# Attention in front of a feed-forward block on one core: the attention's small products placed on parts of TensorE's array

## The chip, the cores and the metric

The kernel runs on one core of one Trainium2 chip. The metric is device time in microseconds. The kernel before took 885.71 us (median of 3 runs, 883.98 to 885.72).

## What is computed

```python
# q, k, v: 8 batches x 8 heads x 576 x 64
kv  = einsum('bhsd,bhse->bhde', k, v)
out = einsum('bhsd,bhde->bhse', q, kv)
rms = sqrt(mean(out * out, axis=-1, keepdims=True) + 1e-06)
x   = out / rms * g_norm                 # then heads side by side: 8 x 576 x 512
h   = (x.transpose(0, 2, 1) @ U) @ V     # U: 576 x 32, V: 32 x 576, a mix along the sequence
u   = x + h.transpose(0, 2, 1)
y   = u + maximum(u @ w_ch1, 0) @ w_ch2  # 512 -> 2048 -> 512
```

The inputs are float32; U, V and the two weights come as 64-bit floats and are decoded to float32 on the chip.

## The kernel before

**The feed-forward block.** The 8 x 576 rows are cut into 9 blocks of 512 (`BLK`). A product in float32r (one pass over TensorE) is made exact enough by splitting both operands into a high and a low part: three products stand for one (`ffn1`, `ffn2`, names `uth`/`utl` for u, `ws` for weights, `hhl` for the hidden layer). The first three blocks (`NSTD`) are computed plainly; the other six, two at a time, with a Strassen scheme, whose weight forms stream from DRAM through `ring`/`ringw`, with `uT`, `uB` and `entry` as operands. While the first block is computed, the weights of each of the 16 slices are loaded, decoded (`decode`, `decode_w`: one instruction on ScalarE and four on VectorE, then a split) and written back to DRAM.

**The attention.** Heads go in pairs, 4 pairs a batch, 32 in all. A pair's steps, in order:

- `kv_step` (L287): k^T v. 512 of the 576 positions lie in `kv_sb` (four chunks of 128), the last 64 in `kvt_sb`. k and v of both heads stand side by side, so a 128x128 product gives both heads' 64x64 blocks on its diagonal; the other two blocks are waste. Batches 0 and 1 (`NATIVE`) do the tail as a product over 64 rows; later ones split the tail into high and low halves (`tails`) for one float32r product of 256 columns, and add up the two parts while copying the diagonal blocks to `kvb`.
- `out_step` (L316): q times kv. `kvb` is block-diagonal, 128x128, its off-diagonal zero, so five float32 products of 128x128 give both heads. ScalarE squares them into `x`.
- `stats_step` and `mul_step` (L329, L343): the root mean square by a chain of small instructions, and `x` scaled from PSUM.
- `xsplit_step` (L352): `x` split into `xh` (all of it, on ScalarE) and `xl` (four chunks, L136), with the low half of the tail written into the free rows of `xh` (L363).
- `turn_step` (L366): `x` transposed into `ut32`, by TensorE and an identity for batch 0, by VectorE and DRAM for the others.
- `t_step` (L382): x^T U. `u2` holds high and low halves of U, 64 columns, as the weights; nine float32r products over the four or five chunks of `xh` and `xl`.
- `t4_step` (L390): the 64 rows of the result copied to `t4` as float32r, the high part again, and the low part (L395, L396): four groups of 32 rows.
- `mix_step` (L445), for batch 0 `mix_first` and `mix_rest`: `t4` times `v4` (V's high and low parts in matching groups of rows), two products of 288 columns, added to `ut32` (L455).

**What sets the order.** Batch 0 is ordered by the table `PLAN` (tasks sorted by their places), with 12 + 10 products that keep TensorE busy. Batches 1 to 7 are placed by `PAIRS` and `STEPS` at steps of the feed-forward loop: batch 1 in the first block, 2 in the second, 3 and 4 in the third, 5 to 7 in the Strassen part; the last third of the program has no attention left. A scheduler orders the first block and the startup; from the second block on TensorE keeps the written order (`pinned`). One line, L89, records every product. Loads go by one queue (SP); `kv_sb`, `kvt_sb` and `q_sb` have one buffer each, and so has `x`.

Of the kernel before, what the change touches and what calls it, by code (L numbers as in the profile page):

```python
# [10 lines left out]
F32 = mybir.dt.float32  # L11
F32R = mybir.dt.float32r
# [38 lines left out]
PLAN = dict(pair=(0, 7, 13, 13), kv=(0, 0, 0, 0), out=(2, 0, 0, 6), stats=(2, 3, 3, 6), mul=(2, 3, 3, 6), xs=(11, 11, 10, 10), tr=(11, 11, 11, 14), t=(14, 14, 12, 14), t4=(18, 18, 14, 18), mix=(18, 23, 21, 23), mt=(42, 42, 42, 42), uv=6, v4=11, w0=49, w1=45, w2=38, w3=49, x0=49, warm=12, fill0=4, fill1=3, fill2=1, fill3=2, u2=60)  # L51
# [8 lines left out]
def build(ctx: ExitStack, tc: tile.TileContext, kv_in, kvt0_in, kvt_in, q_in, uv_in, g_in, w_in, out):  # L60
# [16 lines left out]
    x_sb = const.tile([P, NT, P], F32, name="x")  # L77
# [3 lines left out]
    u2 = const.tile([P, NT, 2 * R], F32R, name="u2")  # L81
    v4 = const.tile([P, S], F32R, name="v4")
    eps = const.tile([P, 1], F32, name="eps")
    kvb = [const.tile([P, P], F32, name=f"kvb{i}") for i in range(2)]
# [12 lines left out]
    def decode(raw, tmp, n=None):  # L97
# [8 lines left out]
        nc.vector.tensor_scalar(out=tmp, in0=tmp, scalar1=ABS_LO, scalar2=ABS_HI, op0=ALU.max, op1=ALU.min)  # L106
# [34 lines left out]

    def load_kv(b, p):
        if b == 0 and 0 < p:
            if p not in first_kvq:
                first_kvq[p] = weight_slot(f"kvq{p}", [P, 2 * MAIN + S], F32, 8 + p)
            kt = first_kvq[p][:, 0:2 * MAIN]
        else:
            kt = ldp.tile([P, 2 * MAIN], F32, name="kv_sb")
        nc.sync.dma_start(out=kt, in_=kv_in[b, p])
        if b >= NATIVE:  # L150
            tt = ldp.tile([P, 2 * P], F32, name="kvt_sb")
            nc.sync.dma_start(out=tt, in_=kvt_in[b - NATIVE, p])
            loads["t", b, p] = tt
        elif p % 2 == 0:
            if b == 0 and p > 0:
                tt = temps[:, 2 * DM:2 * DM + 2 * P]
            else:
                tt = ldp.tile([P, 2 * P], F32, name="kvt_sb")
            nc.sync.dma_start(out=tt, in_=kvt0_in[b, p // 2])
            loads["t", b, p] = loads["t", b, p + 1] = tt  # L160
        loads["kv", b, p] = kt

    def load_q(b, p):
        if b == 0 and 0 < p:
            if p not in first_kvq:
                first_kvq[p] = weight_slot(f"kvq{p}", [P, 2 * MAIN + S], F32, 8 + p)
            qt = first_kvq[p][:, 2 * MAIN:]
        else:
            qt = ldp.tile([P, S], F32, name="q_sb")
        nc.sync.dma_start(out=qt, in_=q_in[b, p])  # L170
        loads["q", b, p] = qt
# [741 lines left out]
```

## Time and profile before

| | us |
|---|---|
| median of 3 runs | 885.71 |
| profiled execution | 887.76 |
| its span | 885.8 |
| TensorE busy | 854.1 |
| VectorE busy | 637.5 |
| ScalarE busy | 385.2 |
| GpSimd busy | 154.6 |

Busy time counts the union of an engine's instructions. A product's end is drawn some way behind the start of the next one, so a busy TensorE is not one at its peak: the distance of starts tells its pace. In rows of TensorE the form 128*64 means weights of 128 rows and 64 columns, and 128x512 the moving operand. A float32 product leaves two records, a float32r one leaves one.

### The profile page before, as it was taken

How to read it: one execution, taken by the hardware profiler on the slowest of the kernel's cores; microseconds unless marked ns; L12 is line 12 of the kernel's file. 1: busy time of each engine (PE TensorE's matmuls, PEld its weight loads, DVE VectorE, ACT ScalarE, POOL GpSimd, SP SyncE). 2: the span in 40 equal slices, each digit the busy share in tenths (PEclk: the TensorE clock that was granted, in tenths of full speed). 3: DMA queues.
4: the chain of work that ended last, by engine and by line, in shares of the span. 5: the costliest groups of instructions: out<-in, count | busy, mean ns of one | idle time of the engine just before them, and what ended most of it. 6: DMA issues, size and time to landing. Idle time of an engine off the chain costs nothing.

```text
span 885.8 us, 12268 instructions
## 1 busy us (share of the span) xinstructions
PE 854.1 (96%) x4214; PEld 712.8 (80%) x4214; DVE 637.5 (72%) x1032; ACT 385.2 (43%) x673; POOL 154.6 (17%) x155
## 2 busy tenths in 40 slices
PE   7799998999998989999999999999999999999998
PEld 7687886788887878888888887788788888888886
DVE  5999997846437866749895989578756885663584
ACT  4554544333323433445554655445435434432441
POOL 2000037777886600020000000000000000000000
PEclk8899999999998999999999999999999999999999
DMA  9996676566557663158778777777676677566665
GB/s 339 406 417 263 231 246 204 159 191 193 165 161 217 208 187 113 55 177 283 221 246 285 237 225 234 257 226 225 215 207 205 200 237 239 186 194 200 194 206 171
DMA packets 111277, 195.38 MB, mean 221 GB/s; under 512 B 11120, under 2 KB 45424, under 8 KB 109296
## 3 DMA queue, kind: packets, MB, share of 16 engines
q1 hardware_dynamic: 111216, 194.60, 67.9%
q8 instruction: 34, 0.56, 0.3%
q14 instruction: 27, 0.22, 0.1%
HBM read 143.31 MB, written 51.25 MB: 220 GB/s over the span
## 4 chain that ended last, share of the span: by engine, by line
PE 76%; DVE 12%; DMA 7%; issue 3%; ACT 2%; SPq 1%; POOL 0%; DVEq 0%; ACTq 0%
PE y L89 56%; PE h L89 10%; PE pp L89 9%; DMA raw<-w_in 2%; DMA out<-st 2%; DVE dec L109 1%; DMA temps<-kvt_in 1%; DVE hhl L474 1%; DMA q_sb<-q_in 1%; DVE utl L416 1%; DVE dec L111 1%; DVE ws L117 1%; DVE ut L455 1%; DVE xh L363 1%; DVE xt L375 1%
## 5 line engine op out<-in xcount | busy, mean ns | idle before, releaser
L89 PE MATMUL y<-entry,ring 128*128 128x512 f32 x576 | 136.1, 390 | 0.0
L89 PE MATMUL y<-hhl,ws 128*128 128x512 f32 x540 | 134.4, 396 | 0.0
L89 PE MATMUL h<-uth,ws 128*128 128x512 f32 x360 | 124.1, 406 | 3.7 <-DVE hhl L474 3.6
L89 PEld LDWEIGHTS y<-entry,ring 128*128 128x128 f32 x576 | 107.4, 188 | 21.8
L89 PEld LDWEIGHTS y<-hhl,ws 128*128 128x128 f32 x540 | 101.2, 190 | 20.8
L543 DVE TENSOR_TENSOR h<-y,h 128x512 f32<-128x512 f32 x71 | 48.5, 688 | 53.4 <-PE y L89 49.0
L89 PE MATMUL y<-uB,ringw 128*128 128x512 f32 x354 | 86.1, 393 | 0.4 <-DVE st L543 0.3
L89 PEld LDWEIGHTS h<-uth,ws 128*128 128x128 f32 x360 | 69.8, 194 | 20.5 <-DVE hhl L474 6.0
L89 PE MATMUL y<-uT,ring 128*128 128x512 f32 x348 | 82.9, 391 | 0.0
L89 PEld LDWEIGHTS y<-uB,ringw 128*128 128x128 f32 x354 | 65.5, 188 | 14.3 <-DVE st L543 1.3
L89 PEld LDWEIGHTS y<-uT,ring 128*128 128x128 f32 x348 | 64.9, 188 | 13.4 <-ACT h L550 0.3
L89 PE MATMUL h<-utl,ws 128*128 128x512 f32 x180 | 72.0, 400 | 0.0
L587 DVE TENSOR_TENSOR entry<-h,entry 128x1024 fp32r<-128x1024 f32 x36 | 43.9, 1219 | 27.4 <-ACT entry L586 27.1
L473 ACT ACTIVATE hhl<-h 128x512 fp32r<-128x512 f32 x47 | 28.1, 597 | 78.3 <-PE h L89 78.2
L474 DVE SCALAR_TENSOR_TENSOR hhl<-h,hhl 128x512 fp32r<-128x512 f32 x47 | 32.2, 685 | 34.3 <-ACT hhl L473 34.1
L89 PE MATMUL y<-dec,ringw 128*128 128x512 f32 x216 | 55.5, 392 | 0.0
L89 PE MATMUL y<-hhl,ringw 128*128 128x512 f32 x216 | 55.2, 390 | 0.0
L251 POOL TENSOR_TENSOR dec<-dec 128x256 f32<-128x256 f32 x64 | 50.3, 786 | 4.9
L89 PE MATMUL y<-uT,ringw 128*128 128x512 f32 x210 | 50.7, 390 | 0.0
L586 ACT CAST entry<-h 128x1024 fp32r<-128x1024 f32 x36 | 37.9, 1053 | 25.9 <-PE y L89 25.8
L89 PEld LDWEIGHTS y<-hhl,ringw 128*128 128x128 f32 x216 | 40.5, 188 | 8.9 <-DMA ringw<-w2s 0.4
L89 PEld LDWEIGHTS y<-dec,ringw 128*128 128x128 f32 x216 | 40.0, 188 | 8.4 <-DVE dec L584 0.4
(210 smaller groups left out, 1436.1 us busy)
## 6 DMA issues: line engine op xcount, KB each, us to landing
ring<-wd SPq DMA_DIRECT2D x69, 256.0 KB, 3.7
ringw<-wd SPq DMA_DIRECT2D x66, 256.0 KB, 3.6
raw<-w_in SPq DMA_DIRECT2D x30, 512.0 KB, 10.0
wd<-ws SPq DMA_DIRECT2D x15, 1024.0 KB, 4.9
kv_sb<-kv_in SPq DMA_DIRECT2D x29, 512.0 KB, 4.5
ring<-w1s SPq DMA_DIRECT2D x48, 256.0 KB, 3.8
ringw<-w1s SPq DMA_DIRECT2D x48, 256.0 KB, 3.7
ring<-w2s SPq DMA_DIRECT2D x48, 256.0 KB, 4.1
```

The source lines that it names most:

```text
L89: ins = nc.tensor.matmul(*args, **kw)
L109: nc.vector.scalar_tensor_tensor(out=bits, in0=high, scalar=0xC0000000, in1=bits, op0=ALU.bitwise_and, op1=ALU.bitwise_or)
L111: nc.vector.scalar_tensor_tensor(out=bits, in0=low, scalar=29, in1=bits, op0=ALU.logical_shift_right, op1=ALU.bitwise_or)
L117: lo_eng.tensor_tensor(out=lo, in0=src, in1=hi.bitcast(F32), op=ALU.subtract)
L251: nc.gpsimd.tensor_tensor(out=o, in0=in0, in1=in1, op=op)
L363: nc.vector.tensor_tensor(out=xh[TAIL:P, 4], in0=s["x"][0:TAIL, 4], in1=xh[0:TAIL, 4].bitcast(F32), op=ALU.subtract)
L375: nc.vector.transpose(out=xt.rearrange("p k i j -> p i k j"), in_=x.rearrange("p i (k j) -> p i k j", j=32))
L473: nc.scalar.activation(out=hh, in_=h, func=AF.Relu)
L474: nc.vector.scalar_tensor_tensor(out=hl, in0=h, scalar=0.0, in1=hh.bitcast(F32), op0=ALU.max, op1=ALU.subtract)
L543: nc.vector.tensor_tensor(out=out, in0=in0, in1=in1, op=ALU.add)
L586: nc.scalar.copy(out=hi, in_=src)
L587: nc.vector.tensor_tensor(out=lo, in0=src, in1=hi.bitcast(F32), op=ALU.subtract)
```

## The change

- k^T v: each head gets a product of its own, with 64 columns of weights and 64 moving columns, over five chunks of 128 positions (the last one filled with zeros). The two heads write partitions 0 to 63 and 64 to 127 of one bank: two column tiles of the array, in turn. One copy moves both to `kvb`, now 128x64. The separate tails, their loads and their splits are gone; `kv_in` is padded to 640 positions.
- q times kv: each head's 64 rows of q and of `kvb` form a product of 64 rows, five a head, the heads in turn: two row tiles, each with a bank of its own.
- x^T U: `xsplit_step` and the halves of U are gone. `x` in float32 is multiplied by U with 32 columns of weights; each chunk goes to two column tiles, even chunks to tiles 0 and 2, odd ones to 1 and 3, ten products. The four groups of 32 rows then hold partial sums, and one copy moves all to `t4`, float32.
- mix: rows 0 to 63 of `t4` and `v4` give the first 288 columns, rows 64 to 127 the other 288: two row tiles, float32, each contracting the even and the odd partial sum. `v4` holds V itself, not halves, and is cleared at the start.
- `x` gets a second buffer (`x_sb[p % 2]`).
- `PLAN` loses an unused entry and gets `d`: the decoding of weight slices 1 and 2 is placed among batch 0's tasks, and their second VectorE instruction is held in the written order.

The core of the diff:

```diff
-PLAN = dict(... fill3=2, u2=60)
+PLAN = dict(... fill3=2, d=(19.5, 20))
...
-        nc.vector.tensor_scalar(out=tmp, in0=tmp, scalar1=ABS_LO, scalar2=ABS_HI, op0=ALU.max, op1=ALU.min)
+        ins = nc.vector.tensor_scalar(out=tmp, in0=tmp, scalar1=ABS_LO, scalar2=ABS_HI, op0=ALU.max, op1=ALU.min)
+        if held:
+            tc.keep_in_program_order(ins)
...
     def kv_step(b, p):
         m = loads.pop(("kv", b, p))
-        t = loads.pop(("t", b, p))
         pp = bank()
         kb = kvb[p % 2]
-        if b >= NATIVE:
-            both = sc.tile([P, 3 * P], F32R, name="tails")
...
-            mm(pp[:, 0:2 * P], lhsT=both[:, 0:P], rhs=both[:, P:], start=True, stop=False)
-        for i in range(4):
-            mm(pp[:, 0:P], lhsT=m[:, i * P:(i + 1) * P], rhs=m[:, MAIN + i * P:MAIN + (i + 1) * P],
-                             start=(i == 0 and b < NATIVE), stop=(i == 3 and b >= NATIVE))
...
+        for i in range(NT):
+            for lo in (0, D):
+                own = slice(i * P + lo, i * P + lo + D)
+                mm(pp[lo:lo + D, 0:D], lhsT=m[:, own], rhs=m[:, NT * P:][:, own], start=(i == 0), stop=(i == NT - 1))
+        move("kv", p if b == 0 else -1, kb, pp[:, 0:D])
...
-        for i in range(4):
-            mm(big[:, i * P:(i + 1) * P], lhsT=qt[:, TAIL + i * P:TAIL + (i + 1) * P], rhs=kb, start=True, stop=True)
-        small = bank()
-        mm(small[:, 0:P], lhsT=qt[:, 0:P], rhs=kb, start=True, stop=True)
+        x = x0[p] if b == 0 else x_sb[p % 2]
+        heads = [bank() for _ in range(2)]
+        for i in range(NT):
+            lo = (TAIL + i * P) % (TAIL + MAIN)
+            for k, o in enumerate(heads):
+                own = slice(k * D, k * D + D)
+                mm(o[:, i * D:(i + 1) * D], lhsT=qt[own, lo:lo + P], rhs=kb[own], start=True, stop=True)
...
-    def xsplit_step(b, p):
...
     def t_step(b, p):
-        xh, xl = state[b, p]["hl"]
+        x = state[b, p]["x"]
         tp = bank()
-        todo = [(xh, i) for i in range(NT)] + [(xl, i) for i in range(4)]
-        for n, (xx, i) in enumerate(todo):
-            mm(tp[0:2 * R, 0:P], lhsT=u2[:, i, :], rhs=xx[:, i, :], start=(n == 0), stop=(n == len(todo) - 1))
+        for i in range(NT):
+            for c in (i % 2, i % 2 + 2):
+                mm(tp[c * R:(c + 1) * R, 0:P], lhsT=u_sb[:, i, :], rhs=x[:, i, :], start=(i < 2), stop=(i >= NT - 2))
...
-        t4 = t40[p] if b == 0 and p in t40 else sc.tile([P, P], F32R, name="t4")
-        move("t4", p if b == 0 else -1, t4[0:2 * R], tp[0:2 * R, 0:P])
-        nc.scalar.copy(out=t4[3 * R:], in_=tp[0:R, 0:P])
-        nc.vector.tensor_tensor(out=t4[2 * R:3 * R], in0=tp[0:R, 0:P], in1=t4[0:R].bitcast(F32), op=ALU.subtract)
+        t4 = t40[p] if b == 0 and p in t40 else sc.tile([P, P], F32, name="t4")
+        move("t4", p if b == 0 else -1, t4, state[b, p]["tp"][:, 0:P])
...
     def keep_warm(p, n):
         for _ in range(n):
-            mm(spare, lhsT=state[0, p]["t4"], rhs=v4[:, 0:MAIN], start=True, stop=True)
+            mm(spare[:, 0:P], lhsT=state[0, p]["t4"], rhs=v4[:, 0:P], start=True, stop=True)
...
-            mm(mp, lhsT=t4, rhs=v4[:, lo:lo + n], start=True, stop=True)
+            rows = slice(lo // n * D, lo // n * D + D)
+            mm(mp, lhsT=t4[rows], rhs=v4[rows, lo:lo + n], start=True, stop=True)
...
+    ahead = 1 + len(PLAN["d"])
+    for f, place in enumerate(PLAN["d"]):
+        tasks.append((place, lambda f=f: decode_w(1 + f, True)))
```

Two places show how the instructions stand. The first is TensorE between two feed-forward products of the third block, where one pair's mix, the next one's x^T U, q times kv and k^T v stand close together (`pp` is the bank written, `t_` is `t4`, `u_` is U, `kvb` holds kv, `ws` and `hhl` belong to the feed-forward block). Before:

```order
L89 MATMUL pp<-v_101,t_2498 128x288 x2
L89 MATMUL pp<-xh,u_100 64x128 x5
L89 MATMUL pp<-xl,u_100 64x128 x4
L89 MATMUL pp<-kvb_103,q_sb 128x128 x5
L89 MATMUL y<-hhl,ws_568 128x512 x12
L89 MATMUL pp<-tails 128x256
L89 MATMUL pp<-kv_sb 128x128 x4
```

After:

```order
L89 MATMUL pp<-v_102,t_2486 128x288 x2
L89 MATMUL pp<-x_94,u 32x128 x10
L89 MATMUL pp<-kvb_104,q_sb 128x64 x10
L89 MATMUL y<-hhl,ws_567 128x512 x12
L89 MATMUL pp<-kv_sb 64x64 x10
```

The steps keep their places; the nine products of x^T U, the five of q and the five of k^T v are ten each now, and smaller.

The second is VectorE at the end of the startup, where batch 0's last pairs, the first mix (`utl`) and the decoding (`dec`, `raw_156` and `raw_149` are weight slice 1, `raw_167` is slice 2, `ws` the split slice) share the queue. Before:

```order
L347 TENSOR_TENSOR x_128<-y,r_387 128x512
L349 TENSOR_TENSOR x_128<-y,r_387 64x128
L130 CAST st<-pp 64x128
L396 TENSOR_TENSOR st<-y,st 32x128
L106 TENSOR_SCALAR dec<-dec 128x1024
L109 SCALAR_TENSOR_TENSOR dec<-raw_156,dec 128x1024
L136 TENSOR_TENSOR xhl_129<-x_128,xhl_129 128x512
L363 TENSOR_TENSOR xhl_129<-x_128,xhl_129 64x128
L396 TENSOR_TENSOR st<-pp,st 32x128
L107 TENSOR_SCALAR dec<-dec 128x1024
L111 SCALAR_TENSOR_TENSOR dec<-raw_156,dec 128x1024
L109 SCALAR_TENSOR_TENSOR dec<-raw_167,dec 128x1024
```

After:

```order
L319 TENSOR_TENSOR x_128<-y,r_393 128x5x64 x2
L106 TENSOR_SCALAR dec<-dec 128x1024
L109 TENSOR_SCALAR dec<-dec 128x1024
L387 SCALAR_TENSOR_TENSOR utl<-pp,g_sb,uth 128x512
L111 SCALAR_TENSOR_TENSOR dec<-raw_149,dec 128x1024
L387 SCALAR_TENSOR_TENSOR utl<-y,g_sb,uth 128x512
L113 SCALAR_TENSOR_TENSOR dec<-raw_149,dec 128x1024
L119 TENSOR_TENSOR utl<-ut_0_95,uth 128x64
L119 TENSOR_TENSOR utl<-ut_1_96,uth 128x64
L119 TENSOR_TENSOR ws_409<-dec,ws_409 128x4x256
```

The splits of x and the small steps of t4 are gone from between, and slice 1 is decoded to its end before slice 2 begins, where before the two were mixed.

More of the change, by code (lines that the diff above doesn't have):

```diff
@@ L59, in build @@
 @with_exitstack
-def build(ctx: ExitStack, tc: tile.TileContext, kv_in, kvt0_in, kvt_in, q_in, uv_in, g_in, w_in, out):
+def build(ctx: ExitStack, tc: tile.TileContext, kv_in, q_in, uv_in, g_in, w_in, out):
     nc = tc.nc
@@ L75, in build @@
     dram = ctx.enter_context(tc.tile_pool(name="dram", bufs=1, space=bass.MemoryType.DRAM))
-    x_sb = const.tile([P, NT, P], F32, name="x")
+    x_sb = [const.tile([P, NT, P], F32, name=f"x{i}") for i in range(2)]
     ut32 = [const.tile([P, S], F32, name=f"ut32_{c}") for c in range(ND)]
@@ L80, in build @@
     g_sb = const.tile([P, 1], F32, name="g_sb")
-    u2 = const.tile([P, NT, 2 * R], F32R, name="u2")
-    v4 = const.tile([P, S], F32R, name="v4")
+    u_sb = const.tile([P, NT, R], F32, name="u")
+    v4 = const.tile([P, S], F32, name="v4")
     eps = const.tile([P, 1], F32, name="eps")
-    kvb = [const.tile([P, P], F32, name=f"kvb{i}") for i in range(2)]
+    kvb = [const.tile([P, D], F32, name=f"kvb{i}") for i in range(2)]
     pinned = [False]
@@ L140, in build, with first_slot @@
     first_kvq = {}
+    def first_slot(p):
+        if p not in first_kvq:
+            first_kvq[p] = weight_slot(f"kvq{p}", [P, 2 * NT * P + S], F32, 8 + p)
+        return first_kvq[p]
     def load_kv(b, p):
[L143 to L148, printed above, removed]
-        nc.sync.dma_start(out=kt, in_=kv_in[b, p])
-        if b >= NATIVE:
[L151 to L160, printed above, removed]
+        kt = first_slot(p)[:, 0:2 * NT * P] if b == 0 and 0 < p else ldp.tile([P, 2 * NT * P], F32, name="kv_sb")
+        nc.sync.dma_start(out=kt, in_=kv_in[b, p])
         loads["kv", b, p] = kt
     def load_q(b, p):
[L164 to L169, printed above, removed]
+        qt = first_slot(p)[:, 2 * NT * P:] if b == 0 and 0 < p else ldp.tile([P, S], F32, name="q_sb")
         nc.sync.dma_start(out=qt, in_=q_in[b, p])
@@ L618, in build @@
     for _ in range(PLAN["warm"]):
-        mm(spare[:, 0:P], lhsT=kvb[0], rhs=kvb[0], start=True, stop=True)
+        mm(spare[:, 0:P], lhsT=v4[:, 0:P], rhs=v4[:, 0:P], start=True, stop=True)
     nc.scalar.sqrt(out=kvb[0][:, 0:1], in_=kvb[0][:, 0:1])
     x123 = weight_slot("x123", [P, NPAIR - 1, NT, P], F32, 15)
-    x0 = [x_sb] + [x123[:, p] for p in range(NPAIR - 1)]
-    xhl = weight_slot("xhl0", [P, NT + 4, P], F32R, 14)
-    xhl0 = [xhl[:, 0:NT], xhl[:, NT:]]
-    for t in x0:
-        nc.gpsimd.memset(t[TAIL:P, 4, :], 0.0)
-    nc.gpsimd.memset(kvb[1], 0.0)
+    x0 = x_sb[:1] + [x123[:, p] for p in range(NPAIR - 1)]
+    nc.gpsimd.memset(x123[:, 0, 0, 0:1], 0.0)
     make_identity(nc, ident)
-    t40 = {p: st.tile([P, P], F32R, name="st") for p in (1, 2, 3)}
+    t40 = {p: st.tile([P, P], F32, name="st") for p in (1, 2, 3)}
     early = [temps[:, i * DM:(i + 1) * DM] for i in range(2)]
@@ L633, in build @@
     for t in t40.values():
-        nc.gpsimd.memset(t[:, 0:1].bitcast(F32), 0.0)
-    for t in xhl0:
-        nc.gpsimd.memset(t[:, 0, 0:1].bitcast(F32), 0.0)
+        nc.gpsimd.memset(t[:, 0:1], 0.0)
     uvs = weight_slot("uvs", [P, DM], I64, 12)
@@ L661, in uv_step @@
         decode(uvraw, uv)
[L662 to L665 removed]
+        move("u", 0, u_sb, uv[:, 0:NT * R].rearrange("p (i r) -> p i r", r=R))
     def v4_step():
         for n in range(4):
[L669 to L670 removed]
+            for k in (n // 2 * 2, n // 2 * 2 + 1):
+                move("v4", n, v4[n * R:(n + 1) * R, k * VQ:(k + 1) * VQ], uv[k * R:(k + 1) * R, NT * R:])
     tasks = [(PLAN["uv"], uv_step), (PLAN["v4"], v4_step)]
@@ L709, in o @@
         def o():
-            for what in (out_step, stats_step, mul_step, xsplit_step):
+            for what in (out_step, stats_step, mul_step):
                 what(b, p)
```

85 lines of the change are left out of this document (21 added, 64 removed).

## The prediction

> **What bounds the kernel now.** I read first the page's busy times and its chain of work that ended last.
>
> ```profile
> PE 854.1 (96%) x4214; PEld 712.8 (80%) x4214; DVE 637.5 (72%) x1032; ACT 385.2 (43%) x673; POOL 154.6 (17%) x155
> PE 76%; DVE 12%; DMA 7%; issue 3%; ACT 2%; SPq 1%; POOL 0%; DVEq 0%; ACTq 0%
> ```
>
> TensorE is busy for 96% of the span and 76% of the chain runs over it; VectorE has 12% of the chain. Such shares are a mean over stages, so the view by windows comes next (a row: stretch, its length, then busy us of each engine with its instructions, granted clock, DMA share, GB/s).
>
> ```profile
> core 0: us, PE busy (x) PEld busy (x) DVE busy (x) ACT busy (x) POOL busy (x), PEclk, DMA share, GB/s
> 20.00:40.00 20.00, 14.38 (x106) 12.80 (x105) 18.92 (x44) 9.35 (x23) 0.61 (x1) 0.91 1.03 407
> 40.00:100.00 60.00, 57.45 (x264) 47.32 (x264) 56.06 (x76) 31.96 (x50) 0.00 (x0) 0.94 0.84 333
> 100.00:150.00 50.00, 48.73 (x251) 40.05 (x250) 47.32 (x73) 23.19 (x41) 19.46 (x14) 1.00 0.64 225
> 150.00:250.00 100.00, 96.44 (x478) 79.51 (x477) 58.52 (x99) 32.45 (x61) 80.47 (x70) 0.98 0.56 174
> 250.00:350.00 100.00, 91.92 (x490) 77.40 (x489) 65.27 (x136) 36.55 (x82) 42.37 (x37) 0.95 0.59 178
> 350.00:550.00 200.00, 199.67 (x1030) 168.23 (x1030) 158.50 (x283) 100.40 (x183) 5.18 (x4) 1.00 0.69 216
> ```
>
> Three stages: from 20 to 150 us VectorE is full (122.3 of 130 us) with the weight decoding and batches 0 and 1; from 150 to 350 us TensorE leads, with 11.6 us idle and a granted clock of 0.98 and 0.95; from 350 us on TensorE has no gap (199.67 of 200). So a VectorE instruction saved before 150 us is worth up to its length, one saved later only where TensorE waits for it, and a TensorE nanosecond added after 150 us counts in full. 24 of the 32 head pairs (batches 2 to 7) lie after 150 us.
>
> **What a pair costs TensorE now.** The timeline of TensorE, in a stage without gaps (start, length with the drawn-out end, records). The pace is the distance of starts, since the drawn lengths overlap; an fp32 product leaves two records, a float32r one leaves one.
>
> ```profile
> 403.08 0.28 PE L89 MATMUL pp<-tails 128*128 128x256 f32 x1
> 403.19 1.05 PE L89 MATMUL pp<-kv_sb 128*128 128x128 f32 x8
> 404.00 1.63 PE L89 MATMUL pp<-uT,ring 128*128 128x512 f32 x6
> 405.46 1.53 PE L89 MATMUL y<-uT,ring 128*128 128x512 f32 x6
> 406.83 2.89 PE L89 MATMUL y<-uB,ring 128*128 128x512 f32 x12
> 409.56 0.47 PE L89 MATMUL pp<-xh,u 128*64 128x128 f32 x5
> 409.86 0.41 PE L89 MATMUL pp<-xl,u 128*64 128x128 f32 x4
> 410.10 1.33 PE L89 MATMUL pp<-kvb,q_sb 128*128 128x128 f32 x10
> 411.19 1.17 PE L89 MATMUL y<-uB,ringw 128*128 128x512 f32 x4
> ```
>
> A 512-column product takes (409.56 - 406.83) / 12 = 0.227 us. k^T v: 404.00 - 403.08 = 0.92, and the six products behind it take 1.46 instead of 1.37, so 1.02 with its exit. x^T U: 410.10 - 409.56 = 0.54 for 9 records, 0.060 each, with 64 columns of weights. q times kv: 411.19 - 410.10 = 1.09, 0.109 a record, and the same 0.1 behind it: 1.18. The mix:
>
> ```profile
> 291.95 0.43 PE L89 MATMUL pp<-v,t 128*128 128x288 f32 x2
> 292.22 0.47 PE L89 MATMUL pp<-xh,u 128*64 128x128 f32 x5
> ```
>
> 0.27 for two, 0.135 each. With 0.06 for leaving x^T U (its narrow weights are followed by a full load, 0.109 against 0.060), a pair is 1.02 + 1.18 + 0.60 + 0.27 = **3.07 us**.
>
> **The change on TensorE.** Two rows that before already holds say what the parts will cost. First, products of 64 rows (the startup's ident times x and the batch 0 and 1 tails):
>
> ```profile
> 40.04 0.43 PE L89 MATMUL pp<-ident,x 64*128 64x64 f32 x2
> 40.31 0.38 PE L89 MATMUL y<-ident,x 64*128 64x64 f32 x2
> 40.63 0.30 PE L89 MATMUL y<-v,st 128*128 128x64 f32 x1
> ...
> 48.58 1.05 PE L89 MATMUL pp<-kv_sb 128*128 128x128 f32 x8
> 49.56 0.48 PE L89 MATMUL pp<-kvt_sb 64*128 64x128 f32 x2
> 49.98 0.50 PE L89 MATMUL pp<-utl,w1s 128*128 128x512 f32 x1
> 50.31 0.40 PE L89 MATMUL pp<-uth,w1s 128*128 128x512 f32 x1
> ```
>
> Of four records with 64 moving columns and 128 of weights none is quicker than one with 128: the starts are 0.27 apart for two, so over 0.11 each. I read that as the weight load setting the pace, 0.11 for 128 columns and 0.060 for 64. And entering and leaving a 64-row product costs: from 48.58, eight records at 0.109 should end at 49.45 and the two of 64 rows at 49.67, but the second 512 product starts at 50.31, where 49.90 would do: 0.4, which I take as **0.39** a visit. The 64-column block x^T U (form 128*64) was entered 2.73 us after its twelve predecessors began, so without any loss.
>
> The Trainium skill, page "TensorEngine Tiling (Array Packing)", section "Key Properties", says that changing the tiling mode, not just the tile, drains TensorE. The trace agrees for 64-row tiles (0.39 a visit) and not for 64-column ones (0.06). By that rule k^T v and x^T U would pay 0.39 as well.
>
> After, a pair if tiles overlap fully:
> - k^T v: ten products, 20 records, 64 columns of weights, two column tiles in turn: 20 x 0.060 / 2 = 0.60, exit 0.06. Bounds: 0.60 overlapped, 1.20 not.
> - q times kv: 20 records, 128 columns of weights, two row tiles in turn: 20 x 0.111 / 2 = 1.11, visit 0.39. Bounds 1.11 and 2.22.
> - x^T U: ten fp32 products, 20 records of 128 moving columns at 0.109, four column tiles: 0.55, exit 0.06. Bounds 0.55 and 2.18. The float32r split is gone, but an fp32 record streams longer; nothing is gained.
> - mix: two fp32 products of four passes at 0.135: 0.54 side by side, visit 0.39. Bounds 0.54 and 1.08.
>
> Sum 0.66 + 1.50 + 0.61 + 0.93 = 3.70, so **+0.63 us a pair**. Nothing covers it after 150 us: 24 x 0.63 = **+15.1 us**. For the four pairs of batch 1 VectorE sets the pace and I cost them at nothing (2.5 us if that cover is gone); in the startup TensorE has 5.6 of 20 us free, which hides the fp32 first mix.
>
> **The change on VectorE, before 150 us.**
>
> ```profile
> L136 DVE TENSOR_TENSOR xl<-x,xh 128x512 fp32r<-128x512 f32 x30 | 20.9, 697 | 0.0
> L363 DVE TENSOR_TENSOR xh<-x,xh 64x128 fp32r<-64x128 f32 x30 | 12.6, 420 | 0.5
> L396 DVE TENSOR_TENSOR t<-pp,t 32x128 fp32r<-32x128 f32 x29 | 8.2, 281 | 4.5 <-ACT t L395 3.9
> L136 DVE TENSOR_TENSOR u<-uvs,u 128x160 fp32r<-128x160 f32 x1 | 0.4, 425 | 0.0
> L117 DVE TENSOR_TENSOR uvs<-uvs 128x144 fp32r<-128x144 f32 x1 | 0.4, 397 | 0.0
> ...
> kv_sb<-kv_in SPq DMA_DIRECT2D x29, 512.0 KB, 4.5
> ```
>
> Three instructions go per pair, 0.697 + 0.420 + 0.281 = 1.40 us, for eight pairs 11.2; two of U and V, 0.82: 12.0 us. The scaling of x (640 columns in two instructions) and t4's move stay; the new memset stands before the first load lands. The two decodings moved ahead of the first hidden layer issue no DMA; on VectorE's queue they stand behind the last scaling of x and ahead of three utl of the first mix, as they nearly did before: nothing. Against it, a load of k and v of batch 0 grows from 512 KB (and half a 128 KB tail) by 64 KB; five stand ahead of the last early weight, 0.33 MB at the 407 GB/s of that window: 0.8 us. So **-11.2 us**, if TensorE can follow; at worst nothing.
>
> **The waits of 150 to 350 us.** A place:
>
> ```profile
> 277.30 0.69 PE L89 MATMUL pp<-xh,u 128*64 128x128 f32 x4 [2.60 <-ACT xh L124]
> 278.82 0.37 PE L89 MATMUL pp<-xh,u 128*64 128x128 f32 x1 [0.83 <-DVE xh L363]
> ...
> 281.51 0.77 PE L89 MATMUL h<-uth,ws 128*128 128x512 f32 x1
> 282.08 0.63 PE L89 MATMUL h<-utl,ws 128*128 128x512 f32 x1
> ```
>
> TensorE waits 3.4 us for the halves of x and then runs at half pace (0.57 for a 512-column product). The halves vanish, and x gets a second buffer. What is late next is x itself (the square root's chain), the q load and the stores, so not all of 11.6 us idle and 7 us of clock (100 x 0.02 + 100 x 0.05) comes back. I take **-7**; bounds 0 and -18.6.
>
> **Sum.** +15.1 - 11.2 - 7 = -3.1 us. The profiled execution took 887.76 us (span 885.8, 2.0 around it), the median run 885.71; 2.05 apart, and neither has a reason to change. 885.7 - 3.1 = **882.6 us**.
>
> **Rivals.**
> 1. *Two at a time* (slower). An fp32 product's two records go to the same tile; if the second holds up the queue behind it, only two products run at once however many tiles there are: x^T U 1.10, mix 0.81, +0.82 more a pair. 24 x 1.45 - 18.2 = +16.6: 902 us, 908 with batch 1 uncovered. It decides as soon as x^T U takes over 0.9 us. For it: no row of before has two tiles at once. The Trainium skill, page "TensorE: Matmul & The Clock Gate", section "Part 3: Packing small matmuls — row/col tiling", says that matmuls start and end strictly in program order, and also that ones on different tiles run concurrently; that is this rival.
> 2. *Loads one after another* (slower): k^T v 1.20, q 2.22, so +1.71: 24 x 2.34 - 18.2 = +38, 924 us. For it: the weight load sets the pace of these forms.
> 3. *No overlap at all*, the tiles do not do what the change says: 1.20 + 2.22 + 2.18 + 1.08 against 2.80 overlapped, +3.88: 28 x 4.51 - 18.2 = +108, 994 us.
> 4. *Every change of mode drains* (slower): 0.33 more for k^T v and for x^T U, 24 x 0.66 = +15.8, 898 us. Against it: the free entry of 64-column tiles; for it: 32-column tiles are not shown. The rule of the Trainium skill quoted above would bring this.
> 5. *All waits go*: the whole 18.6 instead of 7: 871 us.
>
> **Chances.** Forecast 0.50, with its own range 874 to 891 (0.36 faster, 0.08 within, 0.06 slower); rival 1 0.14, 2 0.10, 3 0.07, 4 0.05, 5 0.14. No change means within 0.2%, 1.8 us, about what a measurement of this kernel can tell. Faster 0.36 + 0.14 = 0.50, same 0.08, slower 0.06 + 0.14 + 0.10 + 0.07 + 0.05 = 0.42. The range takes in the forecast and rivals 1, 4 and 5 and leaves out 2 and 3 (0.17): 866 to 912.
>
> **What would show it.** In the timeline after: a block of ten kv_sb products (20 records) about 0.66 long, x^T U about 0.6 (1.1 says rival 1, 2.2 rival 3), q times kv about 1.5 with its visit (2.6 says rival 2), mix about 0.9; the last decoding on VectorE some 10 us earlier than now; TensorE's idle time between 150 and 350 us near 5 us. The forecast is wrong if a pair costs TensorE over 3.85 us, or if the first block of outputs ends no earlier.

## The result, and the profile after

The changed kernel takes 899.61 us (median of 4 runs, 898.97 to 900.96), the kernel before 884.85 us (4 runs, one more than above, 883.17 to 885.72): a ratio of 1.0171, 95% interval 1.0149 to 1.0193, so slower by 1.7%. The profiled execution took 900.01 us with a span of 898.2; before it was 887.76 and 885.8. So the spans differ by 12.4 us, and the steps below are made against that. The medians differ by 14.8: the execution of before that was profiled is 2.9 us above its median, the one of after 0.4.

The page's busy times and chain of work, after:

```profile
PE 877.0 (98%) x5308; PEld 697.8 (78%) x5308; DVE 556.1 (62%) x839; ACT 351.1 (39%) x597; POOL 148.6 (17%) x143
...
PE 74%; POOL 9%; DMA 7%; DVE 6%; ACT 2%; issue 1%; SPq 0%; DVEq 0%; POOLq 0%; ACTq 0%
```

TensorE is busy 22.9 us longer (877.0 against 854.1), VectorE 81.4 us shorter. VectorE's share of the chain is halved, 6% instead of 12%, and the kernel is slower all the same. GpSimd, which prepares the Strassen weights, now has 9% of the chain where it had none.

The view by windows, after (columns as in the prediction):

```profile
20.00:40.00 20.00, 16.33 (x191) 13.93 (x180) 14.18 (x35) 6.17 (x13) 0.61 (x1) 0.89 1.03 409
40.00:100.00 60.00, 58.25 (x380) 45.93 (x380) 58.04 (x81) 32.81 (x51) 0.00 (x0) 1.00 0.89 341
100.00:150.00 50.00, 50.00 (x280) 38.08 (x279) 42.03 (x58) 19.51 (x29) 22.62 (x18) 1.00 0.64 230
150.00:250.00 100.00, 95.14 (x596) 74.27 (x595) 38.06 (x66) 27.75 (x52) 82.72 (x73) 1.00 0.57 177
250.00:350.00 100.00, 98.54 (x751) 76.86 (x750) 43.55 (x90) 30.18 (x70) 34.13 (x31) 1.00 0.59 176
```

From 150 to 350 us TensorE's idle time fell from 11.6 to 6.3 us, and the granted clock is 1.00 in both stretches. That part went as forecast or better. The next view says where the time was lost. VectorE's addition of the residual to each output of the three plain blocks has a line of its own; its row gives the first and the last start. Before and after:

```profile
L487 DVE TENSOR_TENSOR st<-y,uth x12: 678/692/693, 155.3 to 391.0; 128x512 f32<-128x512 f32 x12
```

```profile
L444 DVE TENSOR_TENSOR st<-y,uth x12: 682/691/692, 151.9 to 391.1; 128x512 f32<-128x512 f32 x12
```

The first block's output comes 3.4 us earlier (151.9 against 155.3). The third block's last output starts at the same moment, 391.1 against 391.0. So in these two executions all gains and losses up to there cancel, and **nearly the whole 12.4 us arise behind it**, in the Strassen part (898.2 - 391.1 = 507.1 against 885.8 - 391.0 = 494.8). This part hardly changes from one profile to another (494.3 to 495.5 us in the kernels below whose Strassen part has only k^T v on tiles, 507.2 in the one that has the blocks of after), so the 2.4 us by which the medians differ further most likely lie ahead of it; no profile shows them. The twelve pairs of batches 5 to 7 stand in it, all but the first k^T v. TensorE is busy for 502.8 us of it instead of 489.2, 13.6 more, and idle for 1.3 less (4.3 instead of 5.6, given up between 550 and 690 us): 13.6 / 12 = 1.13 us more a pair, where the prediction had 0.63.

One whole pair of that part, in the timeline of TensorE, after. The 512-column products between the blocks are the feed-forward block's:

```profile
421.01 0.51 PE L89 MATMUL pp<-v,t 64*128 64x288 f32 x1
421.02 0.51 PE L89 MATMUL h<-v,t 64*128 64x288 f32 x1
421.36 0.40 PE L89 MATMUL pp<-v,t 64*128 64x288 f32 x1
421.37 0.40 PE L89 MATMUL h<-v,t 64*128 64x288 f32 x1
421.70 3.03 PE L89 MATMUL y<-uT,ring 128*128 128x512 f32 x12
424.66 0.80 PE L89 MATMUL pp<-kv_sb 128*64 128x64 f32 x20
425.39 3.02 PE L89 MATMUL y<-uB,ringw 128*128 128x512 f32 x12
428.34 0.85 PE L89 MATMUL pp<-x,u 128*32 128x128 f32 x20
429.12 3.03 PE L89 MATMUL y<-uT,ringw 128*128 128x512 f32 x12
432.08 1.33 PE L89 MATMUL pp<-kvb,q_sb 64*128 64x64 f32 x20
433.34 5.74 PE L89 MATMUL y<-entry,ring 128*128 128x512 f32 x24
439.01 0.51 PE L89 MATMUL pp<-v,t 64*128 64x288 f32 x1
```

And of before the rows that begin and end the same stretch, with the same 60 products in it, and its last block:

```profile
419.44 0.30 PE L89 MATMUL pp<-v,t 128*128 128x288 f32 x1
...
429.55 1.27 PE L89 MATMUL pp<-kvb,q_sb 128*128 128x128 f32 x10
430.58 5.74 PE L89 MATMUL y<-entry,ring 128*128 128x512 f32 x24
436.16 0.30 PE L89 MATMUL pp<-v,t 128*128 128x288 f32 x1
```

From mix to mix it is 439.01 - 421.01 = 18.00 us after and 436.16 - 419.44 = 16.72 before. The 60 products take 60 x 0.227 = 13.62. The pair is therefore 4.38 against 3.10: **+1.28** (the prediction had read 3.07 for before). Over the twelve pairs it is 1.13: in seven of them two blocks stand side by side and share about 0.2 us, as a later example shows. Block by block, with what the products behind it lose:

| block | forecast | its length | lost in the products behind it | together |
|---|---|---|---|---|
| k^T v | 0.66 | 25.39 - 24.66 = 0.73 | 2.95 - 12 x 0.227 = 0.23 | 0.96 |
| x^T U | 0.61 | 29.12 - 28.34 = 0.78 | 2.96 - 2.72 = 0.24 | 1.02 |
| q times kv | 1.50 | 33.34 - 32.08 = 1.26 | 5.67 - 24 x 0.227 = 0.22 | 1.48 |
| mix | 0.93 | 21.70 - 21.01 = 0.69 | 2.96 - 2.72 = 0.24 | 0.93 |

The blocks on row tiles cost what was forecast. Those on column tiles cost 0.30 and 0.41 more, and about half of that lies not in the block but in the products around it. A reader who looks at the blocks' lengths alone misses it. Not all of the 0.23 is new: in before the products behind q times kv on the whole array lost 436.16 - 430.58 - 24 x 0.227 = 0.13 too.

### The profile page after: what moved, and what is told of

Its sections match the earlier page's. It is cut to its first block, busy times and chain, and to the rows that moved or that the text cites. A ratio compares the mean times of both kernels' runs of the same rounds, so it can differ in the third digit from the quotient of the medians.

```text
span 898.2 us, 14046 instructions
## 1 busy us (share of the span) xinstructions
PE 877.0 (98%) x5308; PEld 697.8 (78%) x5308; DVE 556.1 (62%) x839; ACT 351.1 (39%) x597; POOL 148.6 (17%) x143
## 4 chain that ended last, share of the span: by engine, by line
PE 74%; POOL 9%; DMA 7%; DVE 6%; ACT 2%; issue 1%; SPq 0%; DVEq 0%; POOLq 0%; ACTq 0%
PE y L89 56%; PE pp L89 9%; PE h L89 8%; DMA raw<-w_in 4%; POOL dec L237 3%; POOL dec L233 3%; POOL wf L119 3%; ACT dec L118 1%; DMA out<-st 1%; DMA kvq<-kv_in 1%; POOL st L445 1%; DVE utl L369 1%; DMA w1s<-wf 1%; DVE st L471 0%; DVE uT L467 0%
## 5 line engine op out<-in xcount | busy, mean ns | idle before, releaser
L89 PE MATMUL h<-uth,ws 128*128 128x512 f32 x360 | 122.0, 399 | 4.2 <-DVE hhl L431 4.1
L89 PEld LDWEIGHTS h<-uth,ws 128*128 128x128 f32 x360 | 67.5, 188 | 23.2 <-DVE hhl L431 6.9
L237 POOL TENSOR_TENSOR dec<-dec 128x256 f32<-128x256 f32 x64 | 48.5, 758 | 4.8
```

The lines of the kernel that those rows point to most:

```text
L89: ins = nc.tensor.matmul(*args, **kw)
L237: nc.gpsimd.tensor_tensor(out=o, in0=in0, in1=in1, op=op)
```

## Experiments

**Theory** (the prediction's fourth rival): TensorE drains whenever a block on tiles follows or precedes products on the whole array, column tiles included. That it drains means here: the products beside the block lose time beyond their 0.227 us each. **Rivals**: that float32 itself costs the time, whatever the tile; that the small products are slow in themselves; that only 64-row tiles drain.

### Which blocks drain: type and tile

The kernel before has a block with 64 columns of weights that was entered without loss. It is float32r. First the same block in float32, in place:

```diff
-            mm(tp[0:2 * R, 0:P], lhsT=u2[:, i, :], rhs=xx[:, i, :], ...)
+            mm(tp[0:2 * R, 0:P], lhsT=u2[:, i, :].bitcast(F32), rhs=xx[:, i, :].bitcast(F32), ...)
```

> The kernel before, with x^T U's nine 64-column products read as float32 instead of float32r (same data, same tile at column 0, nothing left out). Theory 'precision' (a part of the array drains TensorE when the product is float32, and before's x^T U went free only because it was float32r): the block is entered about 0.32 us after the last full product instead of 0.23, and left with another 0.1 to 0.2; a pair costs 18 records x 0.109 + 0.39 = 2.35 instead of 0.60, 24 x 1.75 = +42, about 927 us. Theory 'rows only' (as the prediction had it: 64-row tiles drain, column tiles do not): entry 0.23, a pair 18 x 0.109 + 0.06 = 2.02, +34, about 919 us.

Measured: 923.31 us (one run; the kernel before on that chip 884.55). The entry of the block:

```profile
481.12 2.45 PE L89 MATMUL y<-entry,ring 128*128 128x512 f32 x10
483.51 1.31 PE L89 MATMUL pp<-xh,u 128*64 128x128 f32 x10
```

Ten 512-column products at 0.227 take 2.27; the block starts 2.39 behind the first of them: 0.12 lost at the door. With the same tile, the same columns and the same place, float32 drains where float32r did not. (The time by itself decides nothing: 923 lies midway between the 927 and the 919 expected.) Second, the block in float32r with 32 columns of weights (the low half of U is left out):

```diff
-            mm(tp[0:2 * R, 0:P], lhsT=u2[:, i, :], rhs=xx[:, i, :], ...)
+            mm(tp[0:R, 0:P], lhsT=u2[:, i, 0:R], rhs=xx[:, i, :], ...)
```

> The kernel before with x^T U by the high half of U alone: nine float32r products with 32 instead of 64 columns of weights, at column 0 (the low half of U is left out). Theory "type" (a float32r product at column 0 is done in the mode of the whole array, whatever its columns): the block is entered after 0.227 us, as with 64 columns. Rival "columns" (32 columns are a mode of their own and drain, 64 are not): entered after 0.32 us, and the block and its exit lose about 0.33 us together.

Measured: 886.02 us (one run).

```profile
404.64 2.88 PE L89 MATMUL y<-uB,ring 128*128 128x512 f32 x12
407.36 0.46 PE L89 MATMUL pp<-xh,u 128*32 128x128 f32 x5
```

Twelve products take 407.36 - 404.64 = 2.72 = 12 x 0.227: no loss. Fewer columns do not drain as such. Third, the mix of the changed kernel in float32r, still on two row tiles (T and V are rounded to float32r, their low bits are left out):

```diff
-    v4 = const.tile([P, S], F32, name="v4")
+    v4 = const.tile([P, S], F32R, name="v4")
...
-        t4 = ... sc.tile([P, P], F32, name="t4")
+        t4 = ... sc.tile([P, P], F32R, name="t4")
```

> The changed kernel with t4 and v4 rounded to float32r, so that the mix on two row tiles is float32r (it leaves out the low bits of T and V). Theory 'precision': the mix's visit no longer drains, entry 0.23 and exit near 0.23; a pair costs about 0.14 + 0.05 instead of 0.885, 24 x 0.69 = -17, about 883 us. Theory 'mode' (any change of the tile's size drains, whatever the type): entry 0.32, exit as in the changed kernel, a pair 0.885 - 0.34 (half the passes) - about 0.13 = 0.42 to 0.55, 24 x 0.4 = -9, about 890 us.

Measured: 891.43 us (one run), 8.2 us less than the changed kernel; the theory "mode" had asked for 9, the theory "precision" for 17.

```profile
656.15 1.75 PE L89 MATMUL y<-uB,ringw 128*128 128x512 f32 x7
657.84 0.40 PE L89 MATMUL pp<-v,t 64*128 64x288 f32 x1
657.84 0.40 PE L89 MATMUL h<-v,t 64*128 64x288 f32 x1
658.16 1.65 PE L89 MATMUL y<-uB,ringw 128*128 128x512 f32 x6
```

Seven products take 1.69 instead of 1.59, so this block drains in float32r too. Both products start at once, and yet the block takes 0.32; the two products of before, one behind the other on the whole array, took 0.27. "Float32 itself" falls as a rule: what all three runs and the changed kernel share is that every block on tiles drains, with one exception, the float32r product at column 0. Why that one is free stays open; a float32r product on another column tile was not tried.

### What a visit costs: the same products in two visits

```diff
+    def kv_first(b, p):
+        m = loads["kv", b, p]
+        pp = loads["half", b, p] = bank()
+        for i in range(2):
...
-        for i in range(NT):
+        for i in range(0 if half is None else 2, NT):
...
+            if name == "kv" and b > 1:
+                at(base, lambda: kv_first(b, p))
+                base += 1
+                at(base, what)
...
```

> The changed kernel with the ten k^T v products of the pairs of batches 2 to 7 issued as four and six, with feed-forward products between the two; the same products on the same tiles. Theory "visits" (TensorE drains each time a block on tiles stands between products on the whole array; the block of k^T v lost 0.33 us to it): 24 pairs x 0.33 = 8.0 us more than the changed kernel's 899.6, so 907.6, and each of the two blocks is entered after 0.32 instead of 0.227 us and left with 0.335. Rival "products" (the loss belongs to the small products themselves, whatever stands beside them): no more than 1 us of difference, 899.6.

Measured: 905.53 us (4 runs, 903.31 to 906.80), ratio to the kernel before 1.0243 [1.0215, 1.0271]; 5.9 us over the changed kernel, where 8.0 were expected for 24 more visits. One k^T v in its two visits:

```profile
177.02 0.45 PE L89 MATMUL pp<-kv_sb 128*64 128x64 f32 x8
177.40 0.50 PE L89 MATMUL h<-uth,ws 128*128 128x512 f32 x1
...
180.35 0.57 PE L89 MATMUL pp<-kv_sb 128*64 128x64 f32 x12
180.85 1.89 PE L89 MATMUL y<-hhl,ws 128*128 128x512 f32 x7
```

The first visit lasts 0.38 for 8 records, the second 0.50 for 12; with 0.23 around each it is 0.61 + 0.73 = 1.34 against 0.96 in one visit (the 0.23 is the reading of the table above). No product was added, so **a visit costs 0.38 us by itself**. The row of the outputs:

```profile
L454 DVE TENSOR_TENSOR st<-y,uth x12: 679/692/693, 152.3 to 393.6; 128x512 f32<-128x512 f32 x12
```

The Strassen part takes 905.0 - 393.6 = 511.4, 4.3 us over the changed kernel's 507.1. The 12 visits more would be 12 x 0.38 = 4.6; three of the second halves come to stand beside x^T U and share a part. The visits ahead of 393.6 us cost less than that, about 2 us for twelve; there TensorE has some idle time to give up. "The small products are slow in themselves" asked for no difference and falls. Blocks on tiles that stand side by side share part of the price, as the changed kernel shows where x^T U is followed by q times kv at once:

```profile
410.55 0.85 PE L89 MATMUL pp<-x,u 128*32 128x128 f32 x20
411.33 1.33 PE L89 MATMUL pp<-kvb,q_sb 64*128 64x64 f32 x20
412.59 1.67 PE L89 MATMUL y<-uB,ringw 128*128 128x512 f32 x6
```

The two last 412.59 - 410.55 = 2.04; the twelve products ahead of them lose 0.09 and the twelve behind 0.17, so 2.30 in all, against 1.02 + 1.48 = 2.50 apart.

### Back to the whole array, part by part

The changed kernel with q times kv as five products on the whole array, `kvb` block-diagonal again:

```diff
-            for k, o in enumerate(heads):
-                own = slice(k * D, k * D + D)
-                mm(o[:, i * D:(i + 1) * D], lhsT=qt[own, lo:lo + P], rhs=kb[own], start=True, stop=True)
+            mm(big[:, i * P:(i + 1) * P] if i < 4 else small[:, 0:P], lhsT=qt[:, lo:lo + P], rhs=kb, ...)
```

> The changed kernel with q times kv undone: kvb block-diagonal 128x128 again, five full products a pair. Theory 'visits' (what a pair pays over the forecast is the switching, not the tiles' pace): the block costs 1.18 instead of 1.46, 24 x 0.28 = -6.7, less where it stands beside another tile block whose drain it shared (about 8 pairs, 0.2 each): -5, about 894.5 us. Theory 'records' (twice as many small records are the cost): 20 records become 10, 1.26 becomes 0.63 or less, 24 x 0.6 = -14, about 885 us.

Measured: 891.08 us (4 runs, 890.42 to 892.02), ratio 1.0075 [1.0056, 1.0094], 8.5 us less than the changed kernel.

```profile
584.69 1.52 PE L89 MATMUL y<-uT,ring 128*128 128x512 f32 x6
586.05 1.27 PE L89 MATMUL pp<-kvb,q_sb 128*128 128x128 f32 x10
587.08 1.64 PE L89 MATMUL y<-uB,ring 128*128 128x512 f32 x6
```

Six products take 1.36 = 6 x 0.227, so the block is entered free, and it lasts 1.03 where the tiles needed 1.26: ten records at 0.103 each, against ten pairs of records side by side at 0.126, and no visit. Its row of outputs:

```profile
L446 DVE TENSOR_TENSOR st<-y,uth x12: 680/691/692, 147.2 to 386.6; 128x512 f32<-128x512 f32 x12
```

The Strassen part takes 890.2 - 386.6 = 503.6, 3.5 us less than the changed kernel's; 12 x (1.48 - 1.16) = 3.8 would be expected (1.16 is what the same block takes in the kernel before by the same reading, 1.03 and 0.13 behind it). That bears out the theory "visits", not "records", which asked for twice as much. The rest of the gain, 4.7 us, is there at the first output already (147.2 against 151.9); the whole-array form also changes the instructions that take the squares and scale x, and what of it brings those 4.7 us was not tried. Next, the kernel before with the k^T v tiles alone, everything else as it was (the main lines):

```diff
-        for i in range(4):
-            mm(pp[:, 0:P], lhsT=m[:, i * P:(i + 1) * P], rhs=m[:, MAIN + i * P:MAIN + (i + 1) * P], ...)
...
+        for i in range(NT):
+            for lo in (0, D):
+                own = slice(i * P + lo, i * P + lo + D)
+                mm(pp[lo:lo + D, 0:D], lhsT=m[:, own], rhs=m[:, NT * P:][:, own], ...)
+        for lo in (0, D):
+            move("kv", p if b == 0 else -1, kb[lo:lo + D, lo:lo + D], pp[lo:lo + D, 0:D])
```

> The kernel before with one part of the change alone: k^T v on two column tiles over five chunks of 128, the tails gone; q times kv, x^T U and the mix as before. Theory "visits": TensorE pays 0.93 us a pair for k^T v instead of 1.02, 24 x 0.09 = 2.1 us less, and the split and the adding up of the tails (two or three VectorE and one ScalarE instruction a pair from batch 2 on) no longer hold anyone up, up to 5 us of TensorE's idle time: 878 to 883. Rival "the vector work was not in the way" (the waits of 250 to 350 us are for the halves of x alone): 883 to 885, and the waits for x halves unchanged.

Measured: **876.66 us** (7 runs, 875.09 to 881.57), ratio 0.9927 [0.9902, 0.9952]: faster than both kernels, and a little better than the 878 to 883 expected. Its windows and its row of outputs:

```profile
150.00:250.00 100.00, 98.35 (x543) 80.44 (x542) 47.39 (x83) 33.50 (x66) 82.65 (x72) 1.00 0.54 170
250.00:350.00 100.00, 95.99 (x633) 79.20 (x632) 57.71 (x123) 41.48 (x99) 37.30 (x33) 1.00 0.63 191
```

```profile
L456 DVE TENSOR_TENSOR st<-y,uth x12: 680/692/692, 154.6 to 379.5; 128x512 f32<-128x512 f32 x12
```

The Strassen part takes 874.3 - 379.5 = 494.8 us, just what it took before: on TensorE the tiles gain nothing here, 0.96 against 1.04 a pair at best. All of the gain lies ahead of it, 379.5 against 391.0 (the two profiled executions differ by 11.5 us, the medians by 7.3). TensorE is idle for 5.7 us from 150 to 350 instead of 11.6, with the clock at 1.00 instead of 0.98 and 0.95. What went is the splitting and adding up of the tails on VectorE and ScalarE, and the tails' own loads; the run does not part the two. The rival falls: the split of x is still there, and yet TensorE's waits for the halves of x from 150 to 400 us shrink from 2.6 and 1.9 us to 0.3. With a second buffer for x:

```diff
-    x_sb = const.tile([P, NT, P], F32, name="x")
+    x_sb = [const.tile([P, NT, P], F32, name=f"x{i}") for i in range(2)]
```

> The kernel of the run with the k^T v tiles alone, and two buffers for x in place of one (the buffer of t4 moved to the identity's place to make room). If the single x buffer held up q times kv's squares, waits for x fall and it is 1 to 4 us faster than that kernel; if the waits for x are the chain of the root mean square itself, the two agree within 1 us.

Measured: 878.07 us (5 runs, 875.57 to 879.41), ratio 0.9923 [0.9896, 0.9951]; 1.4 us from the run before, within what the runs of each spread. A second buffer brings nothing that can be measured here.

```profile
L456 DVE TENSOR_TENSOR st<-y,uth x12: 682/691/692, 153.8 to 381.8; 128x512 f32<-128x512 f32 x12
```

These runs make a ladder from before to after (on different chips, on which the kernel before took 884.0 to 884.9): k^T v on tiles 884.0 to 876.7, a second x 878.1, x^T U and mix on tiles (with the early decoding) 891.1, q on tiles 899.6. So **-7.3, +1.4, +13.0, +8.5**: one part of the change gains, and two lose more.

### What VectorE's time is worth

The changed kernel with three unused VectorE instructions a pair put back in batches 0 and 1, as large as those that the change had removed:

```diff
+    def ballast(b, p):
+        x = state[b, p]["x"]
+        t = sc.tile([P, 4, P], F32R, name="ballast")
+        nc.vector.tensor_tensor(out=t, in0=x[:, 0:4], in1=x[:, 1:5], op=ALU.subtract)
...
-            for what in (out_step, stats_step, mul_step):
+            for what in (out_step, stats_step, mul_step) + ((ballast,) if b == 1 else ()):
```

> The changed kernel with three VectorE instructions a pair put back for batches 0 and 1, of the sizes that the change removed (1.40 us a pair, 11.2 in all), their results unused. Theory 'loads' (the startup now ends on the weight loads, so most of the VectorE time saved there was already idle): at most the 3.4 us come back by which the first block ends earlier than before, +2 to +4, about 902 to 903.5 us. Theory 'VectorE' (VectorE sets the pace up to 150 us): +9 to +11, about 909 to 911 us.

Measured: 907.36 us (4 runs, 906.36 to 909.50), ratio 1.0254 [1.0232, 1.0277]; 7.8 us over the changed kernel. The profiled execution, 909.50, is the slowest of the four, 2.1 us above their median.

```profile
L452 DVE TENSOR_TENSOR st<-y,uth x12: 687/692/692, 154.1 to 400.5; 128x512 f32<-128x512 f32 x12
```

The first output comes 2.2 us later (154.1 against 151.9), though 11 us of work were added ahead of it. Of these, 5.0 stand ahead of 40 us, where VectorE was busy for 23.3 of the 40 us and had room for them; the 5.7 behind that point are what the 2.2 can come from. The larger part, 400.5 - 391.1 - 2.2 = 7.2 us, arises in the second and third blocks, where nothing was added; the Strassen part is as before (907.7 - 400.5 = 507.2). The waits of TensorE from 263 to 395 us, those of VectorE and of ScalarE from 280 to 296, and the window behind them:

```profile
PE h L89 <- DVE hhl L439: 3.6, 2, 3.3
```

```profile
DVE r L310 <- ACT ta L309: 2.8, 1, 2.8
```

```profile
ACT dec L118 <- POOL dec L237: 2.4, 1, 2.4
```

```profile
295.00:305.00 10.00, 9.42 (x59) 6.90 (x60) 2.89 (x6) 3.80 (x8) 5.12 (x5) 0.71 0.57 181
```

One wait of 3.3 us stands out. Followed back: TensorE waits for the low half of the hidden layer on VectorE, VectorE stood 2.8 us for a square root on ScalarE, and that stood in ScalarE's queue behind a cast that waited 2.4 us for GpSimd, which prepares the Strassen weights. Behind the wait the clock is 0.71 for 10 us, 2.9 us more. It looks as if a delay of a few us early on put GpSimd's work and a pair's statistics on top of each other later; with one profile of this kernel that is argued and not shown.

Then x^T U and the mix on tiles in batches 0 and 1 alone, where VectorE is full, and as before from batch 2 on, together with the k^T v tiles:

```diff
+        if b < NATIVE:
+            x = state[b, p]["x"]
+            for i in range(NT):
+                for c in (i % 2, i % 2 + 2):
+                    mm(tp[c * R:(c + 1) * R, 0:P], lhsT=u32[:, i, :], rhs=x[:, i, :], ...)
```

(In this kernel and the three behind it x has one buffer, and in batch 1 the next pair's x already stands there when x^T U reads it; the work is the same, its values are not the reference's.)

> The kernel of the run with the k^T v tiles alone; in batches 0 and 1, where VectorE sets the pace, x^T U and the mix are done on tiles in float32, without the split of x; from batch 2 on, where TensorE sets the pace, they stay on the whole array in float32r. Theory "the vector work is worth its time before 150 us only": the first block of outputs is stored 3 to 6 us earlier than with the k^T v tiles alone and the rest is as there, 871 to 874 against 876.7. Rival "the loads of the weights bound the startup" (VectorE's time is not what sets the first block's end): within 1.5 us of 876.7.

> The kernel of the run before this one (x^T U and the mix on tiles in batches 0 and 1 alone), and the two decodings of weight slices 1 and 2 placed among batch 0's tasks as in the changed kernel. If the decoding on VectorE is late for the first hidden layers, 1 to 3 us faster than without; if the loads of the weights set its time, the same within 1 us.

Measured: 894.93 us (6 runs, 892.92 to 896.72), far outside both ranges expected, and 893.63 us (6 runs, 889.06 to 899.42), the same within the spread. The float32 U and V stood in the room of weight slice 14 until batch 1 was done, and TensorE's waits up to 150 us have one large new row, for a weight slice (of the first of the two):

```profile
PE h L89 <- ACT ws L116: 13.1, 1, 13.1
```

So the two were made again with U and V in the room that the halves of x leave free:

```diff
-    vu = weight_slot("vu", [P, S + NT * R], F32, 14)
+    v32 = sc.tile([P, S], F32, name="v32", tag="xh")
+    u32 = sc.tile([P, NT, R], F32, name="u32", tag="xl")
```

> The same as the run with x^T U and the mix on tiles in batches 0 and 1 alone, with the float32 U and V kept in the room of the halves of x, which is free until batch 2 (in the place of weight slice 14 that slice's load ran into them and held up the weights). Theory "the vector work is worth its time before 150 us only": the first block of outputs is stored 3 to 6 us earlier than with the k^T v tiles alone, 871 to 874 against 876.7. Rival "the loads of the weights bound the startup": within 1.5 us of 876.7.

> The kernel of the run before this one and the two decodings of weight slices 1 and 2 placed among batch 0's tasks as in the changed kernel: 1 to 3 us faster than without if the decoding on VectorE is late for the first hidden layers, the same within 1 us if the loads of the weights set its time.

Measured: 875.77 us (6 runs, 873.27 to 880.18), ratio 0.9914 [0.9888, 0.9941], 19 us less for that one move, and 878.55 us (6 runs, 875.75 to 880.30), ratio 0.9932 [0.9908, 0.9955]. Their first outputs:

```profile
L472 DVE TENSOR_TENSOR st<-y,uth x12: 678/691/692, 150.9 to 377.0; 128x512 f32<-128x512 f32 x12
```

```profile
L474 DVE TENSOR_TENSOR st<-y,uth x12: 680/691/693, 155.9 to 383.5; 128x512 f32<-128x512 f32 x12
```

In the profile the first of the two has its first output 3.7 us earlier than the kernel with the k^T v tiles alone (150.9 against 154.6), which the theory asked for; the medians are 0.9 us apart, which the rival asked for. The second, with nothing but two decodings in another place, has it at 155.9 and is 2.8 us slower by the medians, which neither side of its expectation had. But the profiled execution of the first is its fastest (873.27), that of the second its slowest (880.30), and executions of one kernel spread over 5 to 7 us here; so these single profiles cannot say what the order is worth. Nor is the work taken away free of a price: batch 1's four pairs pay for x^T U and the mix on tiles, by the table 4 x (1.02 + 0.93 - 0.64 - 0.27) = 4.2 us as an estimate (0.64 and 0.27 in the kernel before). This stays inconclusive: net of that price, 11 us less of VectorE's work brought between 1 and 4 us.

## Why the prediction was wrong

**The step that failed** is "The 64-column block x^T U (form 128*64) was entered [...] without any loss", from which column tiles were taken as free (exit 0.06). What was read there is true; it was a property of that float32r product, not of its tile. The row that bore on the new blocks was the other one, 0.39 for the 64-row products, which were float32. With a visit at 0.38 instead of 0.06 for k^T v and x^T U the pair comes to 4.34, against 4.38 measured. The prediction had this as its fourth rival, at 898 us and with a chance of 0.05: its mechanism is what the runs show. That its time is only 1.6 us off is luck in part, since three other terms were off and nearly cancel: its pairs would have cost 24 x 1.29 = 31.0 us, 3.9 more than measured, the first stage gave 7.8 less than forecast, and the waits 4.3 more. The Trainium skill, page "TensorEngine Tiling (Array Packing)", section "Key Properties", had said it: a change of tiling mode drains TensorE. The runs agree, for column and row tiles, float32 and float32r, at 0.38 us a visit for k^T v, and show the one exception.

**A second term failed**: VectorE's relief before 150 us, -11.2 in the sum and -3.4 measured. The terms against the profiled spans:

| term | forecast | measured | from |
|---|---|---|---|
| 24 pairs on TensorE | +15.1 | +27.1 | 24 x 1.13, the twelve pairs of the Strassen part taken for all |
| VectorE before 150 us | -11.2 | -3.4 | first output |
| waits and clock | -7 | -11.3 | the rest |
| sum | -3.1 | +12.4 | |

The rest can be read directly as well: between the first and the last of the twelve outputs TensorE's idle time falls from 10.2 to 7.0 us and the clock rises from 0.97 to 1.00 (0.03 x 236 = 7), and 1.3 us of idle time go behind them, 11.6 in all.

- **Overlap**: right. Twenty records of k^T v last 0.73, twenty of x^T U on four tiles 0.78; two at a time would have been 1.10 for x^T U. Rivals 1, 2 and 3 fall. The pair of row tiles in the mix starts within 0.01 us, twice, 0.35 apart.
- **q times kv and mix**: right, 1.48 and 0.93 for 1.50 and 0.93.
- **VectorE's relief**: a saved instruction was said to be worth "up to its length" while VectorE is full. But it is full only while it has data. From 10 to 40 us it is busy for 20.2 us instead of 27.2: 7 us of the saving lie there, and VectorE waits instead. From 40 to 100 us it is full again (58.04 of 60), and between 40 and 150 us its work is only 3.3 us less (100.07 against 103.38). The first output comes 3.4 us earlier, and the last split of a weight slice starts 2.5 us earlier (130.5 against 133.0), where some 10 were forecast. The chain of waits of the first 60 us, by line:

```profile
by line: DMA raw<-w_in 63.8%; DMA kvq<-kv_in 16.8%; DVE dec L111 3.9%; ACT dec L103 1.9%; DVE dec L113 1.9%; DVE dec L106 1.7%; SPq L156 1.4%; issue 1.4%; SPq L151 1.4%; SPq L176 1.3%; DVE dec L109 1.0%; SPq L171 0.8%; SPq L593 0.7%; DVE ut
```

The loads of weights and of k, v and q make up 80% of it. The prediction had the row for this, a DMA share of 1.03 in that window, and used it for the 64 KB more of k and v only.

- **"For the four pairs of batch 1 VectorE sets the pace and I cost them at nothing"**: that cover is gone too. TensorE is busy for 50.00 of the 50 us from 100 to 150 and for 58.25 of the 60 us ahead of that, at a clock of 1.00, so it could hardly have followed a larger relief. Four pairs at 1.13 would be 4.5 us, where the prediction had 2.5 for that case (an estimate; no run parts them from the loads).
- **The waits**: right, and larger than forecast, 11.3 us within the bounds of 0 and 18.6. That what is late next eats part of the gain was right too: 6.3 us of TensorE's idle time stay.
- **"The first block of outputs ends no earlier" or "over 3.85 us a pair"**: the second came true, and the first did not. The two signs were for two different terms, and that is what they told apart.
- **Where the gain went**: up to 391 us the earlier first output and the idle time and clock that came back, 3.4 + 10.3 = 13.7 us, pay for the 12 x 1.13 = 13.6 that twelve pairs cost more. Behind that point there is little left to give back, 1.3 us, and twelve pairs more pay almost in full.

## What to carry to other kernels

A block of small products on array tiles between products on the whole array cost about 0.4 us for the visit here, so tiles pay only where the block saves more than that, or where several such blocks can stand side by side; count the visits before the products. Undo a change with several parts one part at a time: here the part that touched TensorE least, k^T v on tiles, was the one that gained, through the vector work and the loads that it spared. And before a saved instruction on a full engine is put down as a gain, look at what that engine waits for next, above all at a DMA share near 1.

## What was not expected of the hardware

- Two float32r products side by side on row tiles took longer (0.32 us, and the drain) than the same two one after the other on the whole array (0.27).
- Products of 64 rows and 64 moving columns on two row tiles are no cheaper than one of 128 rows and 128 columns: 1.26 us for twenty records against 1.03 for ten.
- A wait of 3.3 us of TensorE was followed by 10 us at a granted clock of 0.71, in a kernel whose other windows from 255 to 345 us show 0.95 and 1.00.
